# First batch of a fused attention and MLP kernel: q loaded and cast in two halves, weights gated on a later cast, and 32x32 array tiles in place of diagonal copies

## The chip, the cores and the metric

The kernel runs on one core of one Trainium2 chip. The metric is the device time of one execution in microseconds (us), and the median of several executions is quoted. Most executions of a kernel agree closely, but some are slow: an execution more than 1.5% above the fastest of the same kernel is called slow. A verdict is a ratio: the mean time of one kernel's fast runs over that of the other's fast runs of the same rounds. It is therefore not quite the ratio of the medians quoted beside it. The 95% interval follows it in brackets, and "same" means that the kernels are within 2%.

The profiled span is about 1.7 us shorter than the time of the same execution (275.0 against 276.75). Times inside an execution are counted from the span's start.

The engines are named as in the profile. PE is TensorE (matrix products), PEld is its weight load, DVE is VectorE, ACT is ScalarE and POOL is GpSimd. A line number such as L300 is a line of the kernel whose profile is shown. The changed kernel is longer, so the same statement has another number there.

## The reference, cut to what matters

Eight batches go through Nystrom attention with 8 heads, 576 rows and 32 landmarks, and the result goes through an MLP with a squared ReLU.

```python
def sm(a, b):                                   # softmax of scaled scores
    s = scale * np.matmul(a, b.transpose(0, 1, 3, 2))
    s = s - np.max(s, axis=-1, keepdims=True)
    e = np.exp(s)
    return e / (np.sum(e, axis=-1, keepdims=True) + 1e-09)
q_lm, k_lm = ...                                # means over segments of 18 rows
A, Bm, C = sm(q, k_lm), sm(q_lm, k_lm), sm(q_lm, k)
Z = Bm.transpose(0, 1, 3, 2) / (norm1 * norm_inf + 1e-06)
for _ in range(6):
    Z = 2 * Z - Z @ Bm @ Z                      # pseudo-inverse, 32x32 for each head
attn = A @ Z @ C @ v
# ---- then, for all 4608 rows of 512:
h = x @ w_in                                    # 512 -> 2048
r = np.maximum(h, 0.0)
return (r * r) @ w_out                          # 2048 -> 512
```

## The kernel before

The kernel computes attention of batch b+1 while the MLP of batch b keeps TensorE busy. Only batch 0's attention has nothing to hide behind, so the first 28 us are a chain of small steps. The parts that the change and the argument touch follow, with cuts marked.

Batch 0 is loaded in float32 through SyncE's queue (k, the tails, then q). Everything else goes through one software queue on GpSimd, in program order: w_in, v of batch 0, the rest of w_in, and q and k of batch 1. The first of these waits for the cast of batch 0's k.

```python
            eng.dma_start(
                X[nm + "raw"][:], src[b, :, 0:NC4 * P, :].rearrange("h (p c) d -> p h c d", c=NC4)
            )
# ... (cut: in prepare, batch 0)
            if b == 0:
                X["cast"] = nc.vector.tensor_copy(X[nm][:, 0:2, :, :], raw[:, 0:2, :, :])
                nc.scalar.copy(X[nm][:, 2:4, :, :], raw[:, 2:4, :, :])
                continue
            nc.vector.tensor_copy(X[nm][:], raw)          # batch 1 and later
# ... (cut: start of batch 0)
            prepare(0, ("k",))
            load_rest(X["cast"])                          # w_in, v, k and q of batch 1, w_out
            warm(6)                                       # dummy matmuls
```

The 32x32 matrices of the inverse lie four on a partition axis of 128 and two beside each other. For a product with a 128x128 stationary operand they are first spread onto a block diagonal, which is a copy on DVE.

```python
        def spread(dst, src):
            nc.vector.tensor_tensor(dst[:], src.unsqueeze(2).to_broadcast([P, 2, 4, M]),
                                    blk_bf[:].unsqueeze(1).to_broadcast([P, 2, 4, M]), ALU.mult)

        def products(diagonal, moving):
            n = moving(0).shape[-1]
            res = ntile([P, 2, n])
            for qd in range(2):
                nc.tensor.matmul(res[:, qd, :], lhsT=diagonal[:, qd, :, :].rearrange("p a m -> p (a m)"),
                                 rhs=moving(qd), start=True, stop=True)
            return res

        def joint_step(old, diagonal):

            nv = products(diagonal, lambda qd: old[:, qd, :, :].rearrange("p z m -> p (z m)"))
            new = newt.tile([P, 2, 2, M], BF16, tag="EY", name="EY")
            last = twice_less(new[:].rearrange("p q z m -> p q (z m)"),
                              old[:].rearrange("p q z m -> p q (z m)"), nv[:])
            nd = newt.tile([P, 2, 4, M], BF16, tag="ED", name="ED")
            spread(nd, new[:, :, 0, :])
            return new, nd, last
```

At the end of batch 0's attention the matrix WT is ready. It is multiplied with w_in in four steps. Each result G is copied by ACT and DVE, the MLP starts on the first of them, and squares of the MLP (`gT`) follow on DVE. The cast of batch 1's k has to come after the copy of G number 0 ("kpin"), and that of its q after the third square. Where exactly they stand in DVE's order is decided when the kernel is built, by a scheduler that estimates times; on the chip that order is fixed.

```python
            if first:
                lo = nc.scalar.copy(dst[:, 0, :], g[0])
                last = nc.vector.tensor_copy(dst[:, 1, :], g[1])
                tc.declare_no_dep(last.ins, lo.ins, reason="other columns and banks")
                if n == 0:
                    X["kpin"] = last
# ... (cut: in the loop over f, 16 tiles of the hidden layer)
            square = mlp_in(b, f, AT, G, gT)
            if (b, f) == (0, 2):
                loaded[0]["qpin"] = square
                prepare_next(1)
```

The softmax here doesn't subtract the row's maximum and nothing guards it: scores larger than these inputs give would overflow.

## Time and profile before

| | before |
|---|---|
| time, median of 3 runs | 276.53 us (275.73 to 277.11) |
| profiled span | 275.0 us |
| TensorE busy | 254.4 us, 93% |
| last q of batch 0 lands | 11.92 us |
| WT of batch 0 copied | 26.38 to 26.81 us |
| last output tile of batch 0's MLP copied ("T4" below) | 72.24 us |

Landing times come from the trace's DMA records. T4 is the end of the fourth copy of an output tile. I use it below to split an execution into the part that batches 0 and 1 decide and the rest.

The page's first two parts show each engine's busy time and the busy tenths in 40 equal slices of 6.9 us each. They are from the kernel before.

```profile
PE 254.4 (93%) x2975; PEld 153.9 (56%) x3013; DVE 175.0 (64%) x486; ACT 157.4 (57%) x273; POOL 43.0 (16%) x66
...
PE   2879999899997999999999999999999999999994
```

The next lines are DVE's timeline of the front of the kernel before. The columns are the start in us, the duration, the engine, the line, the operation, output<-input and its shapes, how many instructions the row joins, and in brackets the idle time before it with what ended that.

```profile
11.95 0.69 DVE L180 CAST nat<-raw 128x1024 bf16<-128x1024 f32 x1 [1.28 <-DMA raw<-in_q_dram]
...
18.28 0.29 DVE L305 SCALAR_TENSOR_TENSOR EY<-EY,n 128x128 bf16<-128x128 bf16 x1 [0.33 <-PE n L300]
18.60 0.29 DVE L293 TENSOR_TENSOR ED<-EY,blk_bf 128x256 bf16<-128x256 bf16 x1
...
19.27 0.28 DVE L305 SCALAR_TENSOR_TENSOR EY<-EY,n 128x128 bf16<-128x128 bf16 x1
...
20.26 0.29 DVE L305 SCALAR_TENSOR_TENSOR EY<-EY,n 128x128 bf16<-128x128 bf16 x1
```

The cast of q waits 1.28 us for its load. A step of the inverse takes 1.0 us from L305 to L305, and each contains a diagonal copy (L293) of 0.29 us in the serial part.

The same view further on shows where batch 0 hands over to batch 1.

```profile
26.38 0.42 DVE L546 CAST WT<-n 128x256 bf16<-128x256 f32 x1 [0.38 <-PE n L543]
27.34 0.69 DVE L570 CAST G<-g 128x512 bf16<-128x512 f32 x1 [0.54 <-PE g L563]
27.95 0.68 DVE L570 CAST G<-n 128x512 bf16<-128x512 f32 x1
28.84 0.69 DVE L183 COPY nat<-raw 128x2048 bf16<-128x2048 bf16 x1 [0.21 <-DMA raw<-in_k_dram]
29.45 0.68 DVE L570 CAST G<-n 128x512 bf16<-128x512 f32 x1
```

The cast of batch 1's k (L183) stands between the copies of G number 1 and number 2, and it already waits 0.21 us for its data. If everything before it becomes faster while the data do not, it waits longer, and the copies behind it in DVE's order wait too.

The last lines are TensorE's timeline of the kernel before in the thirteenth slice, in the middle of batch 2's attention.

```profile
82.42 0.20 PE L300 MATMUL n<-y,UD 128*128 128x32 bf16 x2
82.47 0.22 PE L421 MATMUL n<-ident_bf,an 128*128 128x128 bf16 x1
84.23 0.38 PE L421 MATMUL n<-ident_bf,an 128*128 128x128 bf16 x4 [1.54 <-issue]
```

Five transposes in a row are cut apart after the first: TensorE stands still for 1.54 us, and the releaser is given as "issue", so the profile shows nothing that it waited for. The tile and its operands are the same for all five.

### The profile page before, as it was taken

Reading aid. Unit: us, or ns where it says so; the run is one execution under the profiler, and the core shown is the slowest. Engines: PE = TensorE matmul, PEld = TensorE weight load, DVE = VectorE, ACT = ScalarE, POOL = GpSimd, SP = SyncE. Lnnn points to the kernel's source line nnn. Section 1 sums busy time; section 2 is a strip of 40 time slices with the busy share of each in tenths; the row PEclk is TensorE's granted clock in tenths of the full one; section 3 lists DMA queues with packets and bytes.
Section 4 is the critical chain, followed back from the end, with each engine's and each line's share of the span. In section 5 each row is a group of like instructions: output and inputs, shape, how many; then the busy total and the mean of one; then the engine's idle time right before and its main releaser. Section 6 shows DMA issues by size and latency. Waiting matters only on the chain.

```text
span 275.0 us, 7164 instructions
## 1 busy us (share of the span) xinstructions
PE 254.4 (93%) x2975; PEld 153.9 (56%) x3013; DVE 175.0 (64%) x486; ACT 157.4 (57%) x273; POOL 43.0 (16%) x66
## 2 busy tenths in 40 slices
PE   2879999899997999999999999999999999999994
PEld 1664576356653666546654665556645665466444
DVE  3488988567794469746794569656964759545100
ACT  2452887356944567357835667367916675567211
POOL 3844233310410102201220102200000000000000
PEclk9998999999999999999999999999999999999999
DMA  7999999997599966999899979993741111111032
GB/s 196 246 204 197 204 204 187 208 205 110 75 152 146 177 99 96 159 110 172 129 167 104 176 104 141 176 179 73 135 100 38 41 38 41 63 54 42 16 99 76
DMA packets 69776, 35.32 MB, mean 128 GB/s; under 512 B 37360, under 2 KB 64240, under 8 KB 69744
## 3 DMA queue, kind: packets, MB, share of 16 engines
q0 software_dynamic: 37696, 17.17, 54.2%
q1 hardware_dynamic: 26800, 8.39, 23.9%
q10 hardware_dynamic: 5248, 9.31, 11.5%
q8 instruction: 23, 0.38, 0.5%
q14 instruction: 9, 0.07, 0.1%
HBM read 36.70 MB, written 9.44 MB: 168 GB/s over the span
## 4 chain that ended last, share of the span: by engine, by line
PE 72%; DVE 17%; DMA 3%; ACT 3%; issue 3%; SPq 1%; DVEq 0%; ACTq 0%
PE ops L620 21%; PE h L591 18%; PE n L620 8%; DMA raw<-in_q_dram 3%; DVE ra L404 3%; PE g L563 3%; DVE gT L598 3%; DVE an L411 2%; ACT r L597 2%; PE n L239 2%; PE n L300 2%; PE n L421 1%; DVE nat L183 1%; PE n L440 1%; PE ops_4785 L620 1%
## 5 line engine op out<-in xcount | busy, mean ns | idle before, releaser
L597 ACT ACTIVATE r<-h 128x576 bf16<-128x576 f32 x128 | 81.7, 653 | 34.1 <-PE h L591 28.8
L591 PE MATMUL h<-AT,G 128*128 128x288 bf16 x512 | 83.2, 286 | 0.7 <-ACT r L597 0.3
L598 DVE TENSOR_TENSOR gT<-r 128x576 bf16<-128x576 bf16 x128 | 57.8, 454 | 40.5 <-ACT r L597 39.5
L620 PE MATMUL ops<-w_out_bf,gT 128*128 128x512 bf16 x284 | 79.5, 379 | 0.9
L620 PEld LDWEIGHTS <-gT 128*128 128x128 bf16 x592 | 53.4, 97 | 40.7 <-issue 6.9
L591 PEld LDWEIGHTS <-G 128*128 128x128 bf16 x512 | 45.7, 98 | 19.6 <-issue 1.4
L620 PE MATMUL n<-w_out_bf,gT 128*128 128x512 bf16 x104 | 28.0, 379 | 1.2 <-issue 1.1
L577 DVE CAST G<-g 128x1024 bf16<-128x1024 f32 x14 | 17.2, 1225 | 14.9 <-PE g L563 14.9
L575 ACT CAST G<-g 128x1024 bf16<-128x1024 f32 x14 | 14.2, 1012 | 10.8 <-PE g L563 10.8
L629 ACT COPY o_sb<-ops 128x512 f32<-128x512 f32 x19 | 11.1, 585 | 6.9 <-PE ops L620 4.4
L379 PEld LDWEIGHTS <-T 128*128 128x128 bf16 x256 | 11.9, 100 | 3.8 <-issue 0.2
L425 ACT COPY AT<-n 128x576 bf16<-128x576 bf16 x9 | 5.8, 639 | 13.8 <-PE n L421 11.4
L411 DVE TENSOR_TENSOR an<-EA,rra 128x640 bf16<-128x640 f32 (+2 forms) x18 | 13.3, 740 | 0.0
L404 DVE TENSOR_REDUCE ra<-EA 128x20 f32<-128x640 f32 (+2 forms) x18 | 13.0, 723 | 0.0
L84 POOL DMA_DIRECT2D qkt<-in_k_dram x7 | 5.2, 750 | 48.2 <-PE n L249 31.7
L103 POOL DMA_DIRECT2D vm<-in_v_dram x8 | 7.1, 885 | 31.8 <-PE n L440 29.7
L94 POOL DMA_DIRECT2D raw<-in_k_dram x7 | 6.5, 930 | 32.2 <-DVE ED L293 18.9
L239 PEld LDWEIGHTS <-nat 128*128 128x128 bf16 x256 | 8.8, 97 | 4.6 <-DVE nat L180 1.3
L383 ACT ACTIVATE EA<-n 128x512 f32<-128x512 f32 x16 | 9.7, 607 | 1.7 <-PE n L379 1.7
L214 PEld LDWEIGHTS <-nat 128*128 128x128 bf16 x96 | 7.2, 113 | 6.0 <-DVE nat L180 4.8
L300 PEld LDWEIGHTS <-ED 128*128 128x128 bf16 x64 | 5.2, 98 | 9.1 <-DVE ED L293 5.5
L383 ACT ACTIVATE EC<-n 128x512 bf16<-128x512 f32 x16 | 9.6, 603 | 0.7 <-PE n L379 0.7
(179 smaller groups left out, 333.5 us busy)
## 6 DMA issues: line engine op xcount, KB each, us to landing
out_dram<-o_sb ACTq DMA_DIRECT2D x31, 256.0 KB, 3.8
vm<-in_v_dram POOLq DMA_DIRECT2D x8, 512.0 KB, 15.5
raw<-in_k_dram POOLq DMA_DIRECT2D x7, 512.0 KB, 9.9
raw<-in_q_dram POOLq DMA_DIRECT2D x7, 512.0 KB, 14.7
w_in_bf<-in_moe_w_in_dram POOLq DMA_DIRECT2D x4, 512.0 KB, 10.7
w_out_bf<-in_moe_w_out_dram POOLq DMA_DIRECT2D x4, 512.0 KB, 16.2
out_dram<-o_sb ACTq DMA_DIRECT2D x9, 128.0 KB, 2.8
raw<-in_k_dram SPq DMA_DIRECT2D x1, 1024.0 KB, 5.8
```

The source lines that it names most:

```text
L239: nc.tensor.matmul(means[:, ti, p, :], lhsT=src.rearrange("p h d -> p (h d)"), rhs=seg[:, c + (ti if c == NC4 else 0), :], start=(n == 0 a ...
L379: nc.tensor.matmul(sc[:, c, j, :, :], lhsT=X[nm + "T"][:, c, p, :], rhs=BD[:, 1 if nm == "q" else 0, p, 0:64], start=True, stop=True)
L383: nc.scalar.activation((EA if nm == "q" else EC)[:, qd, 0:NC4, :], sc.rearrange("p c j i m -> p c (j i m)"), AF.Exp, scale=SCALE)
L404: nc.vector.reduce_sum(ras[i][:, lo:hi, :], EA[:, i, lo:hi, :].rearrange("p c (h m) -> p c h m", m=M), axis=AX.X)
L411: nc.vector.tensor_tensor(an[:, i, lo:hi, :].rearrange("p c (h m) -> p c h m", m=M), EA[:, i, lo:hi, :].rearrange("p c (h m) -> p c h m", ...
L575: nc.scalar.copy(dst, gg[:])
L577: last = nc.vector.tensor_copy(dst, gg[:])
L591: last = nc.tensor.matmul(h[:, j, 0:HALF], lhsT=G[:, qd, f * P:(f + 1) * P], rhs=AT[:, qd, j * HALF:(j + 1) * HALF], start=(qd == 0), stop ...
L597: nc.scalar.activation(r.rearrange("p (j t) -> p j t", j=2), h[:, :, 0:HALF], AF.Relu)
L598: return nc.vector.tensor_tensor(gT[:, f, o:o + S], r[:], r[:], ALU.mult)
L620: mark[:] = [nc.tensor.matmul(ops, lhsT=gT[:, f, t * P:t * P + P], rhs=w_out_bf[:, f, i * n:i * n + n], start=(f == 0), stop=(f == NF - 1))]
L629: nc.scalar.copy(o_h, ops)
```

## The change

Its intent is to shorten batch 0's chain. The load of q is split into two halves of heads, so that the casts and segment means of the first half run while the second half still moves. The bulk loads wait for a later instruction (the cast of the tails instead of that of k), so that q has the DMA engines longer for itself. The products of batch 0's inverse use 32x32 tiles of the array directly, so the block-diagonal copies go away. The price is 8 small matmuls in place of 2 for each product. The diff, cut to its core:

```diff
-            eng.dma_start(
-                X[nm + "raw"][:], src[b, :, 0:NC4 * P, :].rearrange("h (p c) d -> p h c d", c=NC4)
-            )
+            parts = ((0, H // 2), (H // 2, H)) if b == 0 and nm == "q" else ((0, H),)
+            for lo, hi in parts:
+                eng.dma_start(
+                    X[nm + "raw"][:, lo:hi, :, :],
+                    src[b, lo:hi, 0:NC4 * P, :].rearrange("h (p c) d -> p h c d", c=NC4)
+                )
 ... (casts and segment means in the same halves: cut)
+        def stationary(src, tag):
+            if first:
+                if src.dtype == BF16:
+                    return src
+                res = newt.tile([P, 2, M], BF16, tag="U", name="U")
+                nc.vector.tensor_copy(res[:], src)
+                return res[:]
+            res = (small if tag == "BT" else newt).tile([P, 2, 4, M], BF16, tag=tag, name=tag)
+            spread(res, src)
+            return res.rearrange("p q a m -> p q (a m)")
 ... (cut)
-            n = moving(0).shape[-1]
+            n, w = moving(0).shape[-1], diagonal.shape[-1]
             res = ntile([P, 2, n])
-            for qd in range(2):
-                nc.tensor.matmul(res[:, qd, :], lhsT=diagonal[:, qd, :, :].rearrange("p a m -> p (a m)"),
-                                 rhs=moving(qd), start=True, stop=True)
+            with nullcontext():
+                for qd in range(2):
+                    for a in range(0, P, w):
+                        nc.tensor.matmul(res[a:a + w, qd, :], lhsT=diagonal[a:a + w, qd, :],
+                                         rhs=moving(qd)[a:a + w], start=True, stop=True)
 ... (every spread of the inverse becomes stationary(...): cut)
             prepare(0, ("k",))
-            load_rest(X["cast"])
             warm(6)
 ... (cut)
-            dve(X["qkt"][:], X["qkt32"][:])
+            load_rest(dve(X["qkt"][:], X["qkt32"][:]))
```

More of the change, by code (lines that the diff above doesn't have):

```diff
@@ L179, in prepare @@
             if b == 0:
-                X["cast"] = nc.vector.tensor_copy(X[nm][:, 0:2, :, :], raw[:, 0:2, :, :])
-                nc.scalar.copy(X[nm][:, 2:4, :, :], raw[:, 2:4, :, :])
+                for lo, hi in ((0, H // 2), (H // 2, H)) if nm == "q" else ((0, H),):
+                    nc.vector.tensor_copy(X[nm][:, 0:2, lo:hi, :], raw[:, 0:2, lo:hi, :])
+                    nc.scalar.copy(X[nm][:, 2:4, lo:hi, :], raw[:, 2:4, lo:hi, :])
                 continue
@@ L235, in segment_means @@
             if first:
-                order.sort(key=lambda x: (x[1] // 2, x[0], x[1]))
+                order.sort(key=lambda x: (x[0] // 2, x[1] // 2, x) if nm == "q" else
+                           (0, x[1] // 2, x))
             for n, (p, c) in enumerate(order):
@@ L288, in attention @@
         EY = newt.tile([P, 2, 2, M], BF16, tag="EY", name="EY")
-        ED = newt.tile([P, 2, 4, M], BF16, tag="ED", name="ED")
-        BT = small.tile([P, 2, 4, M], BF16, tag="BT", name="BT")
+        def stationary(src, tag):
[8 more added lines that the diff above has]
+            return res.rearrange("p q a m -> p q (a m)")
         def spread(dst, src):
@@ L314, in inverse_begin @@
             nc.vector.tensor_copy(btc[:], BB[:, 0, :, :])
-            spread(BT, btc[:])
+            BT = stationary(btc[:], "BT")
             n1 = small.tile([P, 2], F32, tag="n1", name="n1")
@@ L321, in inverse_begin, with inverse_first @@
             nc.vector.reciprocal(rc[:], c1[:])
-            return btc, rc
-        def inverse_first(btc, rc):
+            return btc, BT, rc
+        def inverse_first(btc, BT, rc):
             rcb = rc[:, :].unsqueeze(2).to_broadcast([P, 2, M])
@@ L327, in inverse_first @@
             nc.vector.tensor_tensor(EY[:, :, 0, :], nu[:], rcb, ALU.mult)
-            spread(ED, EY[:, :, 0, :])
+            ED = stationary(EY[:, :, 0, :], "ED")
             nc.vector.tensor_tensor(EY[:, :, 1, :], BB[:, 1, :, :], rcb, ALU.mult)
+            return BT, ED
         def joint_step(old, diagonal):
@@ L336, in joint_step @@
                               old[:].rearrange("p q z m -> p q (z m)"), nv[:])
-            nd = newt.tile([P, 2, 4, M], BF16, tag="ED", name="ED")
-            spread(nd, new[:, :, 0, :])
-            return new, nd, last
+            return new, stationary(new[:, :, 0, :], "ED"), last
         def transposed_y(y):
@@ L350, in last_joint_step, with b_times_v @@
             return y, transposed_y(y)
-        def b_times_v(v):
+        def b_times_v(BT, v):
             nu = products(BT, lambda qd: v[:, qd, :])
-            UD = newt.tile([P, 2, 4, M], BF16, tag="ED", name="UD")
-            spread(UD, nu[:])
-            return UD
+            return stationary(nu[:], "ED")
         def newton_step(y, UD, final):
@@ L470, in attention @@
             scores("k", 0)
-            inverse_first(*inverse_begin())
+            BT, ED = inverse_first(*inverse_begin())
             scores("q", 0)
@@ L492, in attention @@
             yield
-            inverse_first(*begun)
+            BT, ED = inverse_first(*begun)
             yield
@@ L529, in attention @@
         for it in range(2):
-            UD = b_times_v(v)
+            UD = b_times_v(BT, v)
             yield
```

## The prediction

> **What bounds it now.** Two regimes. From about 28 us to the end TensorE is near saturated (the 40-slice table: PE 9 tenths in almost every slice; the page: 254.4 of 275.0 us, matmul busy). Before 28 us batch 0's attention is a latency chain. The chain of waits reads: q's load, landing at 11.92 us; the cast (DVE 0.69, ACT 1.05 us); 20 segment-mean matmuls ending 13.55; q0's transposes and their copy to 15.13; softmax and inverse, nearly all DVE, to the copy of WT at 26.38; G copies from 27.34.
>
> **What the change does, from durations in the timeline.**
> 1. Half casts: ACT's last cast shrinks from 1.05 to about 0.55 us, DVE's from 0.69 to about 0.37; half of the means run before the second half lands. Means end about 12.8 instead of 13.55: -0.7 us. Part of this is already limited by the eight warm-up matmuls, which end at 11.91.
> 2. w_in waits for the tails' cast (ends 8.75) instead of k's (ends 7.3). In the one-microsecond windows the DMA moves 345 GB/s from 8 to 10 us and 199 once the casting loads have it alone; [...]a later start leaves q more: it should land 0.3 to 0.5 us earlier (partly the same gain as 1).
> 3. No diagonal copies: BT's 0.29 us hides behind the fp32 column sums; ED goes four times, each about 0.3 us of serial DVE time; UD (0.41 us) becomes a plain cast (about 0.2) twice. About -1.5 us. The last spread (zt) stays. Against it, each product becomes 8 matmuls instead of 2; c_values' small matmuls pass at about 12 ns each[...]. I estimate +0.05 to 0.1 us per product; only two or three of nine products end a wait, the rest hide behind the row sums on DVE. Net about -1.2.
>
> So WT should be ready 1.8 to 2.7 us earlier, about 24 us.
>
> **How much survives.** Little, I think. The software DMA queue is saturated from 8.5 us on, so batch 1's data don't move: its k lands at 28.8 (the cast of k in line 183 waited for it 0.21 us and began at 28.84), its q at 31.6 (cast 31.87). The order on DVE is static: G copies 0 and 1, k's cast, G copy 2, squares. If it stays, DVE reaches k's cast about 2.4 us earlier and stands until 28.8. Behind it wait G copy 2, hence PSUM for the third and fourth G products, and the squares. PE can run ahead by one or two h tiles only (three r buffers). From 28.8 on all goes nearly as before. w_in's last part (lands about 25.3) would also be needed about 26. I keep 0.3 to 1 us of the 2.4.
>
> **Predicted: 275.7 us, range 273.7 to 277.0.** Faster by over 2%: 0.02; within 2%: 0.96; slower: 0.02.
>
> **What would show each step.** Last q half lands near 11.5, means end near 12.8; ED groups of batch 0 gone; joint steps (twice-less to twice-less) about 0.7 us instead of 1.0; WT copied near 24; the cast of batch 1's k beginning still at 28.6 to 29.2 with a wait for its DMA of 2 us or more (0.21 before); w_in's last landing within 0.7 us of before.
>
> **What would make it wrong.** The scheduler may put k's cast behind more of batch 0's work, or PE may have enough independent work: then the full gain stays, 273.9. Or batch 1's k may land later with the gated weights, or 32x32 products cost 0.2 us or more each: then 276.5 to 277.5.

Two reasons that no trace of this case shows are cut from points 2 and 3, and the cuts are marked. What the prediction calls saturated is a DMA share of 1.08 or more in every window of one microsecond from 8 to 29 us of the kernel before, with 198 GB/s moved from 12 to 28.8 us.

## More of the kernel before

TensorE is at 9 tenths nearly throughout from slice 5 on. Two slices before the last are lower: the eighth is 8 and the thirteenth (82.5 to 89.4 us) is 7.

## The result and the profile after

The changed kernel takes 273.42 us (273.25 to 274.08, 4 runs). The kernel before takes 276.82 us over the 4 runs now known (275.73 to 280.01). The ratio is 0.9895 [0.9858, 0.9931], the same within 2%. The profiled span went from 275.0 to 271.5 us. Both numbers of the ratio come from few runs, so both kernels were run again below.

The page of the changed kernel, the same two lines:

```profile
PE 257.7 (95%) x3067; PEld 153.5 (57%) x3067; DVE 173.8 (64%) x482; ACT 157.5 (58%) x274; POOL 42.9 (16%) x66
...
PE   2988899999999999999999999999999999999994
```

TensorE has more work (54 more matmuls in the program; of the 92 more records, 38 are records missing in the first trace), the span is shorter, and the thirteenth slice is now 9.

DVE's timeline of the front of the changed kernel:

```profile
10.44 0.99 DVE L184 CAST nat<-raw 128x512 bf16<-128x512 f32 x2
12.41 0.29 DVE L260 CAST bd_83<-n 64x128 bf16<-64x128 f32 x1 [0.97 <-PE n L244]
...
16.53 0.29 DVE L321 SCALAR_TENSOR_TENSOR EY<-EY,n 128x128 bf16<-128x128 bf16 x1 [0.35 <-PE n L316]
16.73 0.55 DVE L417 TENSOR_REDUCE ra<-EA 128x12 f32<-128x384 f32 x1
17.72 0.29 DVE L321 SCALAR_TENSOR_TENSOR EY<-EY,n 128x128 bf16<-128x128 bf16 x1 [0.44 <-PE n L316]
...
18.90 0.29 DVE L321 SCALAR_TENSOR_TENSOR EY<-EY,n 128x128 bf16<-128x128 bf16 x1 [0.44 <-PE n L316]
```

The q halves land at 9.39 and 10.88 us. The segment means, which L260 copies, end at 12.30 instead of 13.55. The diagonal copies are gone, yet a step now takes 1.18 us, longer than the 1.0 of before, and it waits for TensorE. TensorE's timeline in the same stretch says why:

```profile
16.24 0.24 PE L316 MATMUL n<-EY 32*32 32x64 bf16 x8 [0.53 <-DVE EY L345]
16.41 0.61 PE L392 MATMUL n<-bd_83,T 128*128 128x64 bf16 x8
16.82 0.62 PE L201 MATMUL idle<-bd_81 128*128 128x256 bf16 x2
17.37 0.29 PE L316 MATMUL n<-EY 32*32 32x64 bf16 x8
```

The eight 32x32 products take 0.24 us, but behind them stand eight score matmuls at 0.61 us and two dummies at 0.62, and the next product comes after them in order. They are slow because the clock was halved (at full clock in the kernel before, eight score matmuls took 0.39 to 0.40 us and two dummies 0.38): the granted clock in windows of one microsecond reads 0.70, 0.50, 0.50 and 0.59 from 16 to 20 us. In the kernel before it was 1.00 from 16 to 19 us, 0.87 from 19 to 20 and 0.50 from 20 to 23 us. The loss in either trace, 1 minus the granted clock summed over the windows from 15 to 24 us, comes to 1.71 us, which at half speed is a stretch of 3.4 us. The second profile of this same kernel, shown below, has the steps at full clock (1.00 from 15 to 19 us). Where such a stretch falls, and how many there are, differs between the profiles; the table at the end of the experiments lists them.

The handover to batch 1 in the changed kernel, DVE's timeline:

```profile
24.79 0.42 DVE L558 CAST WT<-n 128x256 bf16<-128x256 f32 x1 [0.38 <-PE n L555]
...
26.36 0.68 DVE L582 CAST G<-n 128x512 bf16<-128x512 f32 x1
27.48 0.69 DVE L582 CAST G<-n 128x512 bf16<-128x512 f32 x1 [0.44 <-PE n L575]
...
28.73 0.69 DVE L582 CAST G<-n 128x512 bf16<-128x512 f32 x1 [0.18 <-PE n L575]
29.33 0.98 DVE L610 TENSOR_TENSOR gT<-r 128x576 bf16<-128x576 bf16 x2
30.24 0.69 DVE L187 COPY nat<-raw 128x2048 bf16<-128x2048 bf16 x1
```

WT is 1.59 us earlier. The cast of batch 1's k (L187) no longer stands between the copies of G number 1 and 2: the builder's order now has it behind all four copies and three squares. It begins at 30.24, without a wait. This is also later than its data, which landed at 29.57, and they landed 0.75 us later than before (28.82).

TensorE's timeline at the place where the kernel before stood still:

```profile
80.57 0.20 PE L316 MATMUL n<-y,ED 128*128 128x32 bf16 x2
80.63 0.44 PE L434 MATMUL n<-ident_bf,an 128*128 128x128 bf16 x5
```

The five transposes now run in one group. The change did not touch this code, nor anything in batch 2.

ACT's timeline gives T4, the fourth copy of an output tile, first in the kernel before and then in the changed kernel:

```profile
71.66 0.58 ACT L629 COPY o_sb<-ops 128x512 f32<-128x512 f32 x1
```

```profile
69.82 0.58 ACT L641 COPY o_sb<-ops 128x512 f32<-128x512 f32 x1
```

So T4 is 1.84 us earlier. The rest, from T4 to the end of the span, went from 202.8 to 201.1 us, and 1.54 us of that is the pause that ends at 84.23 us. Roughly half of the gain in this pair of profiles lies where the change was made, and the other half lies where nothing was changed.

### The profile page after: what moved, and what is told of

Its sections match the earlier page's. It is cut to its first block, busy times and chain, and to the rows that moved or that the text cites. A ratio compares the mean times of both kernels' runs of the same rounds, so it can differ in the third digit from the quotient of the medians.

```text
span 271.5 us, 7312 instructions
## 1 busy us (share of the span) xinstructions
PE 257.7 (95%) x3067; PEld 153.5 (57%) x3067; DVE 173.8 (64%) x482; ACT 157.5 (58%) x274; POOL 42.9 (16%) x66
## 4 chain that ended last, share of the span: by engine, by line
PE 75%; DMA 10%; DVE 10%; ACT 2%; issue 1%; SPq 0%; POOL 0%; DVEq 0%; ACTq 0%
PE ops L632 23%; PE h L603 19%; PE n L632 9%; DMA raw<-in_q_dram 5%; PE g L575 3%; DMA vm<-in_v_dram 3%; DVE gT L610 2%; DMA qkt_94<-in_q_dram 2%; DVE ra L417 2%; PE n L316 2%; PE n L244 2%; PE n L453 2%; PE n L392 2%; DVE an L424 1%; PE n L434 1%; PE ops_4832 L632 1%
## 5 line engine op out<-in xcount | busy, mean ns | idle before, releaser
L632 PE MATMUL ops<-w_out_bf,gT 128*128 128x512 bf16 x304 | 83.2, 379 | 0.1
L632 PE MATMUL n<-w_out_bf,gT 128*128 128x512 bf16 x112 | 29.6, 380 | 0.0
L316 PEld LDWEIGHTS <-ED 128*128 128x128 bf16 x84 | 6.7, 97 | 11.9 <-DVE ED L307 8.2
```

Of the source, the lines that this page charges most:

```text
L316: nc.tensor.matmul(res[a:a + w, qd, :], lhsT=diagonal[a:a + w, qd, :], rhs=moving(qd)[a:a + w], start=True, stop=True)
L632: mark[:] = [nc.tensor.matmul(ops, lhsT=gT[:, f, t * P:t * P + P], rhs=w_out_bf[:, f, i * n:i * n + n], start=(f == 0), stop=(f == NF - 1))]
```

## The experiments

Two theories are to be told apart for each half of the gain.

- For the pause in batch 2: theory A says that it is a wait for instructions, whose place depends on how many instructions stand before it, so that the change removed it by accident. Its rival says that the new front shifted batch 2's attention against the MLP and so removed a real conflict.
- For batch 0 and 1: theory B says that the front gain was kept because the cast of k moved behind more of batch 0's work. Its rival says that the shorter front itself carries through.

Unless said otherwise, every kernel gave the correct result. The kernel before was run on the same chip beside each group. Its medians were 276.82 (first group of four), 277.12 (second), 277.16 (third) and 278.69 us (last single run).

### 1. Padding: the number of TensorE instructions alone

In the kernel before, 54 tiny dummy matmuls are added in the front, where TensorE has spare time. Each is a weight load and a matmul, so TensorE has 108 more instructions, about as many as the change adds (109). In the changed kernel, 74 are added, which makes 257 instructions more than before, that is 256 plus 1 (256 is about the number of TensorE records to one packet of the instruction queue, as the readings at the end of this experiment show).

```diff
+    def filler(n):
+        z = bds[1].rearrange("p a b c -> p (a b c)")
+        for _ in range(n):
+            nc.tensor.matmul(idle[0:32, 0:32], lhsT=z[:, 0:32], rhs=z[:, 0:32],
+                             start=True, stop=True)
 ...
             warm(6)
+            filler(54)          # 74 in the changed kernel
```

> The kernel before, with 54 tiny filler matmuls (32x32 weights, 32 columns, results unused) in TensorE's idle time before k lands: 108 more TensorE instructions, as many as the change adds, and nothing else of the change. Instruction-fetch theory (the 1.54 us stall of TensorE at 82.7 us of the kernel before comes from where its 16 KB instruction fetches fall): the stall is gone and the time falls by 1.3 to 1.8 us, to a ratio near 0.994. Rival (the stall comes from the later timing of batch 0, or is chance): the stall stays, ratio 1.000 +- 0.002. WT of batch 0 copied at 26.4 us as before in either case.

Measured: 275.04 us (274.24 to 275.94), ratio 0.991 [0.9862, 0.9958]. TensorE's timeline of this kernel at the place of the pause:

```profile
83.20 0.20 PE L306 MATMUL n<-y,UD 128*128 128x32 bf16 x2
83.25 0.44 PE L427 MATMUL n<-ident_bf,an 128*128 128x128 bf16 x5
```

The pause is gone, with the old front, the old inverse and even later data: batch 1's k landed at 29.95 and T4 was 73.03. TensorE's list in the built program is that of the kernel before with the 54 pairs put in, so no new order explains it. Against the expectation WT came 0.64 us later (27.45 against 26.81), so the ratio is what the lost pause gives less what a later front costs.

> The changed kernel with 74 tiny filler matmuls in the same idle time: 148 more TensorE instructions, so that its instruction count from batch 1 on differs from that of the kernel before by 256[...]. Fetch theory: a TensorE stall of about 1.5 us without a releaser comes back after batch 2's c_values matmuls (near 79 to 81 us), and the gain over before shrinks from 3.0 to about 1.5 us (ratio 0.994). Rival: no stall, ratio 0.989 as the changed kernel.

Measured: 277.52 us (275.39 to 279.86), ratio 0.9971 [0.9908, 1.0034]. By 74 dummies the changed kernel lost most or all of its advantage, more than the 1.5 us that were expected. TensorE's timeline:

```profile
82.44 0.20 PE L322 MATMUL n<-y,ED 128*128 128x32 bf16 x2
82.49 0.22 PE L440 MATMUL n<-ident_bf,an 128*128 128x128 bf16 x1
85.23 0.61 PE L440 MATMUL n<-ident_bf,an 128*128 128x128 bf16 x4 [2.52 <-issue]
```

The pause is back, between the first and the second of the same five transposes, with 2.52 us. A second one of 2.07 us stands in batch 0's inverse, between the two halves of a product. Not all of the loss is the pause in batch 2: T4 was 72.27, 1.87 us later than in the changed kernel, and the granted clock was half from 84.9 us on for 3.4 us, right behind the pause (0.50 in the windows from 85 to 88 us). In the two profiles of the kernel before no such stretch followed the pause.

What follows: the pause goes and comes with the number of TensorE instructions before it, while the attention of batch 2 is the same. The rival of theory A, that the new front matters, falls.

Why would the number matter? Three readings point to the feeding of instructions, though no run shows the wait itself.

- The DMA part of the page has a queue of kind "instruction". In the kernel before it moved 23 packets, 0.38 MB or about 16 KB each, and TensorE has 5,988 records (matmuls and weight loads). (The load half alone, with the same matmuls, has 6,026, so 38 are missing.) In the changed kernel there are 24 packets for 6,134 records. That makes 262 records to a packet (6,026 over 23) and 256 (6,134 over 24). That a packet holds a block of 256 instructions of TensorE is my estimate from these counts and from the distances in the next reading.
- The pauses stand near one place when their numbers are divided by 256. Counting the instructions of TensorE in the program's own list, they begin at number 1976 (before), 1977 (the load half alone, below), 2233 and 703 (the padded changed kernel), and 447 (the tile half alone, and the changed kernel when run again, below). Two pairs lie exactly 256 apart (1977 and 2233, 447 and 703). Divided by 256, the remainders are 184, 185, 185, 191, 191. In the changed kernel the five transposes begin at number 2083, remainder 35.
- Beside each of the seven pauses that I followed, a packet of that queue started to move, between 1.4 us before the pause began and 0.5 us after, and TensorE resumed 2.3 to 2.5 us after that start in six of them, 3.2 us in one. By these times a pause is short when TensorE still had work for the first part of this time, and long when it did not. The traces of experiments 3 and 5 hold four more pauses of this kind: 0.99, 1.00 and 1.00 us at number 447 again (no_gate, old_order, late_cast_no_warm) and 0.54 us at number 703 (late_cast), all in batch 0 and ended 2.28 to 2.41 us after a packet's start.

The two pages' lines on that queue, first the kernel before and then the changed kernel (packets, MB, share of the 16 DMA engines' time):

```profile
q8 instruction: 23, 0.38, 0.5%
```

```profile
q8 instruction: 24, 0.39, 0.6%
```

Most of these packets stand beside no such pause. By this reading a block would be used up fast where small matmuls follow each other: c_values, with 160 TensorE instructions from 80.36 to 81.16 us in the kernel before, stands just before the paused transposes.

### 2. The two halves of the change, each alone

The first kernel has only the split load, the split casts and the later gate. The second has only the tiles.

```diff
 load_only: the kernel before with
+            parts = ((0, H // 2), (H // 2, H)) if b == 0 and nm == "q" else ((0, H),)
 ... (loads, casts and means in halves)
-            load_rest(X["cast"])
+            load_rest(dve(X["qkt"][:], X["qkt32"][:]))

 tiles_only: the changed kernel with all of the above put back
```

> The two halves of q and the gate on the tails' cast alone; products and diagonal copies as before, so the same TensorE instruction count as before. From the changed trace the load should give 1.25 us at the means (last mean matmul about 12.3 us against 13.55) and the copy of WT at 25.1 us against 26.38. If batch 1's loads took the gain back (my prediction), ratio 0.998 to 1.000; if TensorE's independent work keeps it, ratio 0.995 to 0.996, with the 1.5 us stall near 81 us still there by the fetch theory.

Measured: 277.59 us (276.22 to 279.72), ratio 1.001 [0.9951, 1.0068]. WT was ready at 25.32 (26.81 and 25.62 in the two profiles of the kernel before), but the cast of batch 1's k, which moved only behind G number 2 and one square, began at 29.35 after 0.70 us of waiting. T4 was 72.05. The pause in batch 2 was there, 1.49 us at 84.04.

> The 32x32 products without diagonal copies alone; loads and gate as before. My prediction priced this at 1.2 us on the copy of WT (25.2 us); the changed trace suggests only 0.3 us (26.1 us), because joint steps took 1.18 us there instead of 1.0. By the fetch theory the stall near 82 us is gone as well, so the ratio is 0.993 (0.3 + 1.5 us); without it 0.999.

Measured: 274.59 us (274.12 to 275.36), ratio 0.9895 [0.9849, 0.9942]. The granted clock was full throughout, and the joint steps began at 16.46, 17.18 and 17.90 us, 0.72 us apart. The pause in batch 2 was gone; one of 1.00 us stood in batch 0's c_values, in the chain that was shortened, and one of 0.66 us at 176 us. The cast of batch 1's k stood again between G number 1 and 2 and waited 1.78 us for its data (DVE's timeline). T4 was 71.40.

```profile
28.34 0.69 DVE L183 COPY nat<-raw 128x2048 bf16<-128x2048 bf16 x1 [1.78 <-DMA raw<-in_k_dram]
```

What follows: the load half alone is worth nothing that these runs show. The tile half alone has about the gain of padding alone. Since the tile half carries all of the added matmuls, its ratio cannot be credited to the tiles without experiment 1.

### 3. The order on DVE, and the gate

In the first kernel the changed kernel's order is forced back: the cast of batch 1's k directly behind G number 1, the squares behind the later copies. In the build this came out one place off: the first square stands behind G number 3, where the kernel before has it between number 2 and number 3. The second undoes the gate alone, so that the bulk loads again wait only for batch 0's k.

```diff
 old_order: the changed kernel with
                 if n == 0:
                     X["kpin"] = last
+                if n == 1:
+                    prepare(1, ("k",))
+                pins.append(last)
 ...
-        return nc.vector.tensor_tensor(gT[:, f, o:o + S], r[:], r[:], ALU.mult)
+        with tc.issue_after(pins[2 + min(f, 1)].ins) if b == 0 and f < 4 else nullcontext():
+            return nc.vector.tensor_tensor(gT[:, f, o:o + S], r[:], r[:], ALU.mult)

 no_gate: the changed kernel with
+            load_rest(X["cast"])
             warm(6)
 ...
-            load_rest(dve(X["qkt"][:], X["qkt32"][:]))
+            dve(X["qkt"][:], X["qkt32"][:])
```

> The changed kernel, with VectorE's order of batch 1's k cast put back as in the kernel before: after the second G copy, ahead of the third. TensorE's instruction count is that of the changed kernel. My prediction's mechanism (a cast that stands on VectorE until batch 1's k lands takes the early start back) says: the cast waits 1.5 to 2.5 us for its DMA, batch 2's stages begin 1 to 1.7 us later than in the changed kernel, ratio to before 0.994 to 0.996 instead of 0.989. Rival (TensorE has enough work anyway): ratio unchanged, 0.989 to 0.990.

Measured: 276.02 us (275.46 to 278.56), ratio 0.9951 [0.9914, 0.9988]. DVE's timeline of this kernel:

```profile
25.90 0.68 DVE L582 CAST G<-n 128x512 bf16<-128x512 f32 x1
29.40 0.69 DVE L187 COPY nat<-raw 128x2048 bf16<-128x2048 bf16 x1 [2.82 <-DMA raw<-in_k_dram]
30.01 0.68 DVE L582 CAST G<-n 128x512 bf16<-128x512 f32 x1
```

This is the wait that the prediction had foreseen, 2.82 us long, and G number 2 stands behind it. T4 was 73.59, later than in the kernel before. Later data (k at 29.38 against 28.82) account for 0.56 us of that. For the rest this profile has two things that the kernel before does not have: the late first square kept ACT's buffers full, so that TensorE stood still for 1.74 us, and the granted clock was half from 32.5 to 35.9 us. TensorE's timeline:

```profile
32.46 1.60 PE L606 MATMUL h<-AT,G 128*128 128x288 bf16 x6 [1.74 <-ACT r L612]
```

So old_order overstates what the order alone costs. The profiled execution was the slowest of the seven timed. It has another wait, 2.19 us at 101.92 us for a transposed tile that a DMA brings, so its span of 276.8 us says less than the timed runs.

> The changed kernel with w_in gated on k's cast as before. q's second half should land 0.3 to 0.8 us later and batch 1's k about 0.5 us earlier (28.8 us). Without the gate the scheduler puts batch 1's k cast right after the second G copy, as in the kernel before. If the later place of the cast is what kept the gain: ratio 0.992 to 0.995. If the gate only shuffles transfers: 0.988 to 0.990.

Measured: 274.26 us (274.02 to 275.21), ratio 0.9897 [0.9863, 0.9931]. Without the gate, batch 1's k landed at 28.28, earlier than in any kernel with the later gate. But the builder then put its cast back behind G number 1, and the whole order around it is that of the kernel before. The cast began at 28.31 after 1.12 us of waiting (DVE's timeline). T4 was 71.36, against 70.40 in the changed kernel.

```profile
28.31 0.69 DVE L188 COPY nat<-raw 128x2048 bf16<-128x2048 bf16 x1 [1.12 <-DMA raw<-in_k_dram]
```

The gate's effect on the data is read from the windows of one microsecond (columns: window, its length, busy time and count for each engine, granted clock, DMA share, GB/s). First the kernel before, then the changed kernel:

```profile
10.00:11.00 1.00, 1.00 (x7) 0.75 (x6) 0.54 (x2) 0.61 (x3) 1.00 (x2) 1.00 1.21 260
11.00:12.00 1.00, 0.92 (x5) 0.31 (x3) 0.05 (x1) 0.05 (x1) 1.00 (x3) 1.00 1.22 199
```

```profile
10.00:11.00 1.00, 1.00 (x7) 0.69 (x6) 0.86 (x3) 1.00 (x5) 1.00 (x2) 1.00 1.06 80
11.00:12.00 1.00, 1.00 (x19) 0.81 (x18) 0.43 (x1) 0.52 (x1) 1.00 (x3) 1.00 0.89 168
```

From 10 to 12 us the changed kernel moved 211 KB less (459 against 248). At the 200 GB/s at which the queue then runs, that is about 1 us, an estimate worked out from these rows. It fits the landing of batch 1's k: 28.1 to 28.9 us in seven profiles with the old gate (29.95 in the padded one), 29.3 to 30.0 in six with the new one.

What follows: with the order of before, which no_gate and tiles_only have exactly, the gain in the front is lost in one wait (1.12 and 1.78 us). With the gate undone, the order goes back by itself. So the later gate delays batch 1's data by about 1 us and still comes out ahead (T4 0.96 us earlier, median 0.8 to 1.0 us lower, on different chips), since it also changed the order. Here the indirect effect, which nobody asked for, was the useful one.

### 4. A shorter front still, and both kernels again

The dummy matmuls that run beside batch 0's inverse are removed from the changed kernel (16 of them), and 16 fillers are added in the front so that the number of instructions stays.

```diff
                 f(*args)
-            if first:
-                warm(2)
```

> The changed kernel without the two dummy matmuls after each side job of batch 0's inverse, and with 16 tiny fillers before k lands so that TensorE's instruction count stays that of the changed kernel. If the joint steps of 1.18 us in the changed trace were TensorE working at half clock (scores, two dummies, product in order), they fall to about 0.8 us even at half clock, and WT is ready 0.6 to 1.2 us earlier; the half-clock stretch may last longer. Total: ratio 0.986 to 0.989 if the front still pays, 0.989 if batch 1's loads take it. Rival[...]: steps stay 1.1 to 1.2 us.

Measured: 273.05 us (272.95 to 273.77, 5 runs), ratio 0.9854 [0.9818, 0.989]. The steps of the inverse took 0.67 and 0.75 us at full clock and 0.83 us at half clock, against 1.18, so what stood between the products in TensorE's order had made them long. WT was copied at 23.41, 1.8 us before the changed kernel's 25.21. T4 was 70.13, only 0.27 us earlier, and the total is not separable from that of the changed kernel. This alone does not decide against the rival of theory B, because without the dummies the clock was also low for longer: it was half from 17.4 to 27.6 us, 10.2 us against 3.4 in the changed kernel, so the early WT met slow matmuls (the mean clock was 0.979 to 0.987 in its timed runs, 0.991 to 1.0 in the changed kernel's). The better pair is tiles_only and the second profile of the kernel before (shown next), which have the same order on DVE: WT is 0.88 us earlier in tiles_only, batch 1's k lands 0.21 us later, and T4 is 0.22 us later. So with the early cast a shorter front alone does not carry through, and there the rival falls.

> The kernel before, unchanged, as a null run and for a second trace: ratio 1.000 within 0.004. Fetch theory: a stall without a releaser of 1.3 us or more near 82 us, after batch 2's c_values, again; chance theory: none there. The fetch theory also says that the resumed instruction is the same one.

Measured: 279.92 us (277.06 to 281.28, the slowest of the four counted as slow), ratio 1.0062 [1.0, 1.0125] against the other runs of the very same kernel. That is outside the 0.4% that were expected, so a ratio to this kernel can be off by about 0.6%. The pause was there, longer (TensorE's timeline):

```profile
84.58 0.38 PE L421 MATMUL n<-ident_bf,an 128*128 128x128 bf16 x4 [2.95 <-issue]
```

This profile's T4 was 71.18, 1.06 us earlier than in the first profile of the kernel before: batch 0's q landed at 11.23 and batch 1's k at 28.11.

> The changed kernel, unchanged, for a direct comparison on one chip and a second trace: 273.4 +- 0.6 us, no TensorE stall without a releaser near 80 us. If its batch 0 runs at full clock in this trace, the joint steps take 0.72 us instead of 1.18 and WT is ready about a microsecond earlier; the total should then hardly change.

Measured: 273.29 us (272.87 to 273.77), ratio 0.9854 [0.982, 0.9888]. DVE's timeline of this second profile of the changed kernel:

```profile
15.85 0.29 DVE L321 SCALAR_TENSOR_TENSOR EY<-EY,n 128x128 bf16<-128x128 bf16 x1 [0.35 <-PE n L316]
...
16.58 0.29 DVE L321 SCALAR_TENSOR_TENSOR EY<-EY,n 128x128 bf16<-128x128 bf16 x1
...
17.30 0.29 DVE L321 SCALAR_TENSOR_TENSOR EY<-EY,n 128x128 bf16<-128x128 bf16 x1
```

Here the step takes 0.72 us, as the tiles were meant to make it. Then a pause of 1.59 us came inside batch 0's c_values (TensorE's timeline), so that WT was copied only at 25.82:

```profile
20.75 0.21 PE L453 MATMUL n<-vt,ect 128*32 128x64 bf16 x4 [1.59 <-issue]
```

T4 was 70.48 all the same, 0.08 us from the first profile. Between 25.2 and 25.8 us it does not matter here when WT is ready.

### 5. Both at once: early data and a late cast

If the gate costs 1 us of batch 1's data and the order is what helps, the loads of no_gate with the cast held back by hand should be better than the changed kernel. Three versions were tried, all with the old gate and 16 fillers. Two hold the cast of k behind G number 2 (with and without the dummies beside the inverse). The third has the changed kernel's own order, k behind the third square and q behind the fifth, without those dummies.

```diff
 late_cast, late_cast_no_warm: no_gate with
-                if n == 0:
+                if n == 2:
                     X["kpin"] = last

 late_pins: no_gate with
-                if n == 0:
-                    X["kpin"] = last
 ...
-            if (b, f) == (0, 2):
-                loaded[0]["qpin"] = square
+            if (b, f) in ((0, 2), (0, 4)):
+                loaded[0]["kpin" if f == 2 else "qpin"] = square
                 prepare_next(1)
```

> The changed kernel with w_in gated on k's cast as before (batch 1's k lands at 28.3 instead of 29.4 us), with batch 1's k cast kept behind the third G copy by its pin, and 16 tiny fillers. If the gate costs a microsecond of loading that the later order hides, this is 0.5 to 1 us faster than the changed kernel (272.5 to 273 us). If only the order matters: the same as the changed kernel, 273.4.

Measured: 275.15 us (274.06 to 275.56), ratio 0.9916 [0.988, 0.9952]. Here the cast of k stood behind G number 2 but ahead of number 3 and of the squares. It waited 1.45 us for its data and began at 28.77. T4 was 72.72; the clock was half from 32.5 to 35.9 us in this profile, which may be part of that.

> As late_cast, and without the two dummy matmuls after each side job of batch 0: WT at about 23.5 us. If batch 1's loads set the pace from 28 us on, 272.0 to 272.8 us, hardly better than late_cast; if the front pays in full, 271.5.

Measured: 274.47 us (273.91 to 275.19), ratio 0.9895 [0.9856, 0.9933]. T4 was 71.77. As in every kernel without these dummies, the half-clock stretch was long: 18.0 to 28.2 us (10.2 us, against 10.2 in no_warm_steps and 6.8 in late_pins).

> The later order of the changed kernel with the earlier loads: w_in gated on k's cast as before, batch 1's k cast pinned behind the square of slice 2 and its q cast behind that of slice 4 (where the changed kernel has them), no dummies after the side jobs, 16 tiny fillers. Over all traces so far, the early order starts the last store of batch 0's MLP 43.08 us after batch 1's k lands, and the late order 38.1 to 38.3 us after batch 1's q lands. If that landing sets the pace in the late order too, this kernel (q landing near 31.0 us instead of 32.1) is 0.8 to 1.1 us faster than the changed one: 272.0 to 272.6 us. Rival (the late order is bound by TensorE's own work after 28 us): 273.0 to 273.4, and the distance from the landing grows to 39 us or more.

Measured: 273.66 us (273.24 to 278.65, the highest of them slow), ratio 0.9827 [0.9779, 0.9875] (unclear whether faster by 2%) beside a kernel before at 278.69, which is why its ratio looks better. Its median is 0.2 to 0.4 us above that of the changed kernel in its two measurements. Batch 1's k landed at 28.70 as meant, but a new wait of 1.51 us appeared: TensorE stood at 55.29 us for a copy of G by DVE in a later batch. The clock was half from 18.7 to 25.5 us. T4 was 71.52.

What follows: none of the three beats the changed kernel. Theory B is shown in one direction only. Taking the order away takes the gain (no_gate loses 0.96 us at T4, and old_order loses more, with its disturbances), but giving the order without the gate did not give more, and a half-way order (late_cast) was no better than none (ratio 0.9916 against 0.9897 in no_gate, on different chips). Two of the three kernels also ran longer at half clock, so these runs do not show what early data with a late cast would give at the same clock. A T4 of 71.52 less the wait of 1.51 would be 70.0, but that is arithmetic and not a run.

### All profiles on one table

Times in us. "k1" and "q1" are the landings of batch 1's k and q, "WT" is the end of batch 0's WT copy, and "rest" is the span less T4. "half clock" says where the granted clock was 0.5, the last 2 us of the span left out.

| kernel | order of k's cast | WT | k1 | q1 | T4 | rest | pause after T4 | half clock |
|---|---|---|---|---|---|---|---|---|
| before | G1 | 26.81 | 28.82 | 31.32 | 72.24 | 202.8 | 1.54 | 19.7 to 23.1 |
| before again | G1 | 25.62 | 28.11 | 30.76 | 71.18 | 204.2 | 2.95 | 17.7 to 21.1 |
| before + 54 | G1 | 27.45 | 29.95 | 32.60 | 73.03 | 201.2 | none | 19.8 to 23.2 |
| tiles_only | G1 | 24.74 | 28.32 | 30.98 | 71.40 | 202.2 | 0.66 at 176 us | none |
| no_gate | G1 | 25.26 | 28.28 | 31.00 | 71.36 | 201.1 | none | 22.1 to 25.5 |
| old_order | G1, squares late | 24.76 | 29.38 | 32.08 | 73.59 | 203.2 | none, but a DMA wait of 2.19 | 32.5 to 35.9 |
| load_only | G2, one square | 25.32 | 29.32 | 32.05 | 72.05 | 202.7 | 1.49 | 17.3 to 20.7 |
| late_cast | G2 | 23.99 | 28.74 | 31.48 | 72.72 | 201.1 | none | 32.5 to 35.9 |
| late_cast_no_warm | G2 | 25.26 | 28.94 | 31.64 | 71.77 | 201.1 | none | 18.0 to 28.2 |
| changed | all G, 3 squares | 25.21 | 29.57 | 32.28 | 70.40 | 201.1 | none | 16.4 to 19.8 |
| changed again | same | 25.82 | 29.43 | 32.16 | 70.48 | 201.1 | none | 20.9 to 24.3 |
| no_warm_steps | same | 23.41 | 29.36 | 32.03 | 70.13 | 201.1 | none | 17.4 to 27.6 |
| changed + 74 | same | 27.61 | 30.02 | 32.74 | 72.27 | 205.2 | 2.52 | 23.4 to 26.8, 84.9 to 88.3 |
| late_pins | same | 24.10 | 28.70 | 31.43 | 71.52 | 201.1 | none | 18.7 to 25.5 |

Two regularities stand out. In the five profiles with the early cast and the exact order of before, T4 less k1 is 43.42, 43.07, 43.08, 43.08 and 43.08, although WT differs by 2.7 us: the arrival of batch 1's k sets the pace, and what the front gains beyond it is not paid. (In old_order it is 44.21, with the two disturbances named there.) In the changed kernel, its repeat and no_warm_steps, T4 less q1 is 38.12, 38.32 and 38.10. (For the padded one it is 39.53: there the front was late. For late_pins it is 40.09, of which 1.51 is the new wait.) And the rest is 201.1 to 201.2 us wherever no pause or other wait stands in it. The pause explains the excess in the kernel before within 0.2 us, both times. It explains only 2.5 of the 4.1 us in the padded changed kernel, and 0.66 of 1.1 in tiles_only. In the padded changed kernel the half clock from 84.9 to 88.3 us is the likely remainder: about 3.1 us of it lie behind the pause, and half of that is 1.5 us, an estimate. The 0.4 us in tiles_only were not traced.

## Why the prediction was right or wrong, point by point

"Within 2%" held, and so did its main reason, that little of the front's gain survives. The number was too high by 2.3 us: the median of 273.42 lies 0.3 us below the low end of the range. The pause, which was not in the sum, accounts for that: with the pauses of 1.54 and 2.95 us of the kernel before still in it, the changed kernel would take about 275 to 276.4 us, an estimate, inside the range.

- **"Means end about 12.8".** They ended at 12.30. Part of this is the run, not the change: in the profiles with q in one piece, it landed anywhere between 10.94 and 12.38 us. That the later gate leaves q more of the DMA was my reason for an earlier q. Among the kernels with q in halves, the last half landed at 10.88 and 10.98 us in the changed kernel and at 11.38 in no_gate, which differs by the gate alone: 0.4 to 0.5 us. This agrees with the 0.3 to 0.5 us that I had estimated. How the later gate brings this about is not shown. (Three more profiles with the old gate, which also have fillers, have 11.56 to 11.77.)
- **"Joint steps about 0.7 us".** Right at full clock (0.72 in two profiles), but 1.18 in the first profile, where the clock was half and matmuls of other work stood in TensorE's order.
- **"+0.05 to 0.1 us per product".** Too high for the step that waits for the product: the eight 32x32 matmuls took 0.24 us, the two of before 0.23. For TensorE's own queue it was about right: the next matmul started 0.17 us after the first of the eight, and 0.07 us after the first of the two (full clock in both). The 80 small matmuls of batch 2's c_values start 8 ns apart at full clock (80.36 to 80.97 us in the kernel before), so the six more would be 0.05 us of these 0.10, an estimate. What the rest is was not shown.
- **"WT about 24 us".** It began at 24.79.
- **"Batch 1's data don't move".** Wrong. With the later gate 211 KB less moved from 10 to 12 us, and k landed at 29.4 to 29.6 instead of 28.1 to 28.8. The prediction did name this as a risk. The last part of w_in moved too, from 25.21 to 26.61 us, where I had allowed 0.7.
- **"The order on DVE is static ... If it stays".** This is the step that failed. The order is fixed on the chip, but it is made anew for each build, and the gate changed it. The cast of k began at 30.24 with no wait, where I had foreseen 28.6 to 29.2 with 2 us or more. With the order put back by force, the wait was 2.82 us and the ratio 0.9951; with the exact order of before and no gate, it was 1.12 us and the ratio 0.9897. So the mechanism was right, its size depends on when the data come, and its premise was not right. "The scheduler may put k's cast behind more of batch 0's work" stood under what would make the prediction wrong, and that is what happened. Measured at T4, the gain kept was 1.84 us in the first pair of profiles and 0.70 in the second; I had kept 0.3 to 1.
- **The missing term.** The pause of TensorE in batch 2, 1.54 and 2.95 us in two profiles, was not in the sum at all. It stood in the profile of before as a wait whose releaser is "issue", in a slice with 7 tenths. Padding alone, which changes nothing else in the program, gives 0.991 of the 0.9854 that the change gives in its second measurement, so around 60% of the gain (0.9% of 1.5%) comes from it. This share is rough, because the two ratios were measured on different chips and their intervals are 0.3 and 0.5% wide to each side. Against the first measurement of the change (0.9895) it would be over 80%.

That the kernel before scatters more (275.7 to 281.3 us) than the changed one (272.9 to 274.1) also fits a pause of varying length. That is argued and not shown. The record shows another part of it: of 48 runs of the kernel before with a clock on record, the 27 with a mean clock of 0.991 or more have a median of 276.8 us, and the 21 with 0.988 or less one of 279.3. All ten runs of the changed kernel are at 0.991 or more. One stretch of 3.4 us at half clock brings the mean over 275 us to 0.994, and 0.988 takes 6.6 us of it, an estimate from these clocks. So many runs of the kernel before had more half clock than one such stretch. That a pause brings it on, as in the padded changed kernel, is likely, and not shown.

What stays open: why TensorE pauses at those blocks and not at others, beyond the observation that short instructions precede them; what brings on the further half-clock stretches; and whether the late order with early data would pay without the wait at 55 us and at the changed kernel's clock.

No version clearly beats the changed kernel. The one without the dummies beside the inverse (273.05 us) is not separable from it.

## What to carry to other kernels

Before crediting a change, look in both traces for idle time of the limiting engine that has no releaser and lies far from the edit; when the number of instructions changed, run a control that changes only that number, and read the control's trace too, because it can bring effects of its own (here a stretch of half clock, or a square one place off). A front made faster pays only up to the next thing that sets the pace, here the arrival of the next batch's data, so compare a milestone behind that point (here T4) and not the end of the shortened chain. A statement order that a scheduler makes belongs to the build, so read it from the new build before you reason from the old one.
